# A decode block on one core: VectorE's score loop takes all 32 groups in halves, and the sums free the key slot

## The chip, the cores and the metric

The kernel runs on one core of a Trainium2 chip. The metric is the device time of one execution in microseconds (us), as a median of several runs. 1 MB is a million bytes here; the sizes of single DMAs are in KB of 1024 bytes, as the profile gives them.

## The reference

Four tokens (one for each of B = 4 sequences) pass through two branches that are added. Branch A is attention over a cache: H = 32 heads, S = 4096 cached positions, head width DH = 128, model width D = 512, all float32. Branch B is an MLP; with a single token for each sequence its spatial-shift mixing adds nothing (every shift moves in zeros), so w1 and w2 are not needed. Cut to what is computed:

```
xn  = layernorm(x)
q   = (xn @ wq) by heads
p   = softmax(q . k_cache * DH**-0.5)          # 4 x 32 heads, 4096 positions each
att = (p . v_cache) @ wo
x1  = xn                                        # the shifted mixing is zero for one token
mlp = x1 + gelu(layernorm(x1) @ w3) @ w4
out = x + att + mlp
```

The two caches are 268 MB each; nearly all that the kernel reads is in them, and each element is used once.

## The kernel before, in words

The 128 pairs of sequence and head are taken in NJ = 32 groups of four heads (G = 4). A group's keys are one block of 8.39 MB, 64 KB in each of 128 partitions (R = 128 cached positions of DH = 128 numbers), and its values are another such block. SBUF holds three such slots: two for keys, `ks[0]` and `ks[1]`, used in turn, and one for values, `vs`. The weights borrow the slots: w3 lies in `vs` and wq in `ks[1]` at the start, the values of the last group in `ks[0]`, w4 in `vs` and wo in `ks[1]` at the end.

A group goes through four engines:

- **VectorE (DVE)**, function `scores`, L294 to L330: it fetches the group's query (`qg`, L307) and spreads it over the partitions (`qb`, L308), waits for the keys (`take`, L309), multiplies them in place by the query (L314), sums each row of 128 into a score (`sc`, L315), and finds the negated maximum by head (L319 to L321), which signals `nm`.
- **ScalarE (ACT)**, loop at L335: it waits for `nm`, takes four exponentials into `pw` (L340), signals `go`; later it copies the results out of PSUM (L345, L347) and signals `done`.
- **TensorE (PE)**, function `values`, L367: it takes `go`, signals `expd` (the scores of the group are consumed, L369), waits for the values, and multiplies weights by values (L374, 64 matmuls in the trace's counting) and the normalisers (L379, L381).
- **SyncE (SP)**, L271 to L284, issues nearly all DMAs, in an order written out by hand. SP waits for a semaphore ahead of each load, so a load that is not free to go holds back the ones written behind it.

SP's order is: w3, wq, keys 0; keys 1 (after the q projection has read wq); values 0; keys 2 in two halves; values 1; and from then on keys j+2 and values j+1 in turn. The last loads are values 31 (into `ks[0]`), w4 and wo in five parts. I call the loads k0, k1, ... and v0, v1, ... after their group, and k2a and k2b the halves of k2. Keys j+2 wait for `expd` of group j, which TensorE gives only after VectorE's maxima and ScalarE's four exponentials; values j+1 wait for `done` of group j:

```
load(ks[j % 2], rows(kf, j + 2), f"k{j % 2}", None, EXPD[j])
load(vs, rows(vf, j + 1), "landed", None, DONE[j])
```

On VectorE the groups are not all in the loop. Group 0 is written out ahead of it and works in two halves of R/2 = 64 rows; its first half signals `half`, which frees the first half of the slot for k2a. Group 1 is written out as well, in one piece. Then VectorE waits for k2a (`half_in`, L327) and enters the loop (L329), which takes groups 2 to 31, two in each of 15 iterations, in one piece each:

```
scores([qT[:, 0]], halves=True)
scores([qT[:, 1]])
do.wait("DVE", [half_in])
with nc.Fori(1, NJ // 2, engines=OrderedEngineSet([DVE]), head_slot={DVE: 0}) as j:
```

`take` waits for a semaphore and then lowers it by as much; inside `scores` each instruction waits for the one ahead of it through the semaphore `dve`. `head_slot` says at which slot of a block of instructions the loop's first instruction is placed.

Of the kernel before, what the change touches and what calls it, by code (L numbers as in the profile page):

```python
# [41 lines left out]
AX = mybir.AxisListType  # L42
# [7 lines left out]
PE, DVE, ACT = mybir.EngineType.PE, mybir.EngineType.DVE, mybir.EngineType.Activation  # L50
# [36 lines left out]
def decode_block(ctx: ExitStack, tc: tile.TileContext, x, k, v, wq, wo, w3, w4, out):  # L87
    nc = tc.nc
    B, H, S, DH = k.shape
# [5 lines left out]
    R = G * S // P  # L95
    NG = R // 4
    NJ = B * H // G
# [3 lines left out]
    LAST = NJ - 1  # L101
# [4 lines left out]
    def sb(name, *shape):  # L106
        return consts.tile([P, *shape], F32, name=name)
# [4 lines left out]
    ks = [sb(f"ks{n}", R * DH) for n in range(2)]  # L112
# [11 lines left out]
    gT = sb("gT", NF, B)  # L124
    qT = sb("qT", NJ, DH // HP)
    qg = sb("qg", DH // HP)
    qb = sb("qb", DH)
    sc = [sb(f"sc{n}", R) for n in range(2)]
# [13 lines left out]
    kf = k.rearrange("b h s d -> (b h s d)")  # L142
    vf = v.rearrange("b h s d -> (b h s d)")

    def rows(flat, j):
        n = G * S * DH
        return flat[j * n:(j + 1) * n].rearrange("(p n) -> p n", p=P)

    def blocks4(start, stop, w, m, src):
# [5 lines left out]
    do = Steps(tc)  # L155
    sems = {n: tc.alloc_semaphore(n) for n in (
        "x", "w3", "wq", "k0", "k1", "landed", "last", "w4", "go", "pv", "copied", "poz", "out",
        "half", "half_in", "nm", "dve", "expd", "done")}
    wo_sems = [tc.alloc_semaphore(f"wo{n}") for n in range(5)]
    wo_sb = ks[LAST % 2].rearrange("p (c n) -> p c n", c=WC)  # L160
    wo_cuts = ((0, 16), (16, 24), (24, 28), (28, 31), (31, WC))
# [1 line left out]
    g4 = vs[:, NF * D:NF * D + 4 * 32].rearrange("p (m i) -> p m i", m=4)  # L163

    def load(o, i, sem, by, *after, queue="SP"):
        return do(queue, lambda e: e.dma_start(o, i), *after, done=(sems[sem], 16, by))

    with tc.tile_critical():
# [63 lines left out]
        for c in range(NC):  # L232
            for t in range(4):
                up = lambda e: e.matmul(y[32 * t:32 * t + 32, :FT], x1nT[:, c, :], w3_sb[:, c, t * FT:(t + 1) * FT],
                                        start=(c == 0), stop=(c == NC - 1))
                d = do("PE", up)
# [3 lines left out]
        d = do("DVE", lambda e: e.tensor_mul(u, hs, hs), a)  # L240
        d = do("DVE", lambda e: e.tensor_scalar(u, u, GELU_B, 1.0, op0=ALU.mult, op1=ALU.add), d)
        d = do("DVE", lambda e: e.tensor_mul(u, u, hs), d)
        a = do("ACT", lambda e: e.activation(th, u, AF.Tanh, scale=GELU_A), d)
        d = do("DVE", lambda e: e.tensor_scalar(th, th, 1.0, 0.5, op0=ALU.add, op1=ALU.mult), a)
        d = do("DVE", lambda e: e.tensor_mul(hs, hs, th), d)
        d = do("DVE", lambda e: e.transpose(gt, hs), d)
        gT_ok = do("DVE", lambda e: e.tensor_copy(gT, gt.rearrange("p (m i) -> p m i", i=32)[:, :, 0:B]), d)
# [4 lines left out]
        for c in range(NC):  # L252
            for n in range(2):
                for h in range(G):
                    q = lambda e: e.matmul(pq[n][HP * h:HP * h + HP, :], xnT[:, c, :], wq_h[:, c, n, h],  # L255
                                           start=(c == 0), stop=(c == NC - 1))
                    pq_ok = do("PE", q)
        for n in range(2):
            a = do("ACT", lambda e: e.mul(pw_row[:, n * 4 * DH:(n + 1) * 4 * DH], pq[n], DH ** -0.5), pq_ok)  # L259
        d = do("DVE", lambda e: e.transpose(wide, pw_row), a)  # L260
        pw_ok = do("POOL", lambda e: e.memset(pw, 0.0), d)
        qT_ok = do("DVE", lambda e: e.tensor_copy(
            qT.rearrange("p (b i) n -> p b i n", b=B),
            wide.rearrange("p (i n m) -> p m i n", n=DH // HP, m=32)[:, 0:B]), d)

        EXPD = [(sems["expd"], j + 1) for j in range(NJ)]
        DONE = [(sems["done"], j + 1) for j in range(NJ)]
        HALF = R * DH // 2  # L270
        load(ks[1], rows(kf, 1), "k1", None, pq_ok)  # L271
        load(vs, rows(vf, 0), "landed", None, gT_ok, qT_ok, total_ok)
        half_in = load(ks[0][:, :HALF], rows(kf, 2)[:, :HALF], "half_in", 16, (sems["half"], 1))
        load(ks[0][:, HALF:], rows(kf, 2)[:, HALF:], "k0", None, EXPD[0])
        for j in range(LAST - 1):
            if j > 0:
                load(ks[j % 2], rows(kf, j + 2), f"k{j % 2}", None, EXPD[j])
            load(vs, rows(vf, j + 1), "landed", None, DONE[j])
        last_in = load(ks[(LAST - 1) % 2], rows(vf, LAST), "last", 16, EXPD[LAST - 1])
        w4_in = load(w4_sb, w4.rearrange("(p m) n -> p m n", m=NF), "w4", 16, DONE[LAST - 1])  # L280
        do.wait("SP", [EXPD[LAST]])
        wo_r = wo.rearrange("(p c) n -> p c n", c=WC)
        for (c0, c1), sem in zip(wo_cuts, wo_sems):
            nc.sync.dma_start(wo_sb[:, c0:c1], wo_r[:, c0:c1]).then_inc(sem, 16)  # L284
        d = do("POOL", lambda e: e.memset(g4, 0.0), DONE[LAST - 1])
        g4_ok = do("POOL", lambda e: e.tensor_copy(g4[:, :, 0:B], gT[:, 0:4, :]), d, gT_ok)

        def take(engine, sem, n=1):

            engine.wait_ge(sems[sem], n)  # L290
            engine.sem_inc(sems[sem], -n)  # L291


        def scores(groups, halves=False):  # L294
            n = 0

            def step(i, done="dve"):
                nonlocal n
                if n:
                    i.wait_op(sems["dve"], n, "sem-ge")  # L300
                i.then_inc(sems[done], 1)
                n += done == "dve"

            e = nc.vector
            for s, q in enumerate(groups):
                s = s if len(groups) > 1 else 1 - halves
                step(e.tensor_copy(qg, q))  # L307
                step(e.transpose(qb.rearrange("p (n m) -> p n m", m=HP), qg.unsqueeze(2).to_broadcast([P, DH // HP, HP])))  # L308
                take(e, f"k{s}", 16)  # L309

                w = R // 2 if halves else R
                for c in range(0, R, w):
                    kt = ks[s].rearrange("p (c d) -> p c d", c=R)[:, c:c + w]
                    step(e.tensor_tensor(out=kt, in0=kt, in1=qb.unsqueeze(1).to_broadcast([P, w, DH]), op=ALU.mult))  # L314
                    step(e.reduce_sum(sc[s][:, c:c + w], kt, axis=AX.X), "half" if c + w < R else "dve")  # L315
                if halves:
                    e.wait_ge(sems["half"], 1)
                rm, nm = small[:, s, 0:1], small[:, s, 1:2]
                step(e.reduce_max(rm, sc[s], axis=AX.X))  # L319
                step(e.transpose(tr[s], rm.to_broadcast([P, HP])))  # L320
                step(e.tensor_reduce(nm, tr[s], axis=AX.X, op=ALU.max, negate=True), "nm")  # L321
            take(e, "dve", n)

        do.wait("DVE", [qT_ok])
        scores([qT[:, 0]], halves=True)
        scores([qT[:, 1]])
        do.wait("DVE", [half_in])  # L327
        pairs = qT.rearrange("p (j s) n -> p s j n", s=2)
        with nc.Fori(1, NJ // 2, engines=OrderedEngineSet([DVE]), head_slot={DVE: 0}) as j:  # L329
            scores([pairs[:, s, bass.ds(j, 1)].rearrange("p o n -> p (o n)") for s in range(2)])  # L330


        do.wait("ACT", [pw_ok, rs0])
        ozs = oz.rearrange("p n (j s h) -> p s n j h", s=2, h=G)
        with nc.Fori(0, NJ // 2, engines=OrderedEngineSet([ACT]), head_slot={ACT: 0}) as j:  # L335
            for s in range(2):
                take(nc.scalar, "nm")
                for h in range(G):
                    hp = slice(HP * h, HP * h + HP)
                    i = nc.scalar.activation(  # L340
                        pw[hp, :, 4 * h:4 * h + 4], sc[s][hp, :].rearrange("p (g w) -> p g w", w=4), AF.Exp,
                        bias=small[hp, s, 1:2], scale=1.0, accum_out=rs[hp, h:h + 1])
                i.then_inc(sems["go"], 1)
                take(nc.scalar, "pv")
                nc.scalar.copy(os, pv.rearrange("p (m d) -> p m d", m=4)).then_inc(sems["copied"], 1)  # L345
                take(nc.scalar, "poz")
                nc.scalar.copy(ozs[:, s, :, bass.ds(j, 1)].rearrange("p n o h -> p n (o h)"),  # L347
                               poz[:, 0:2 * G].rearrange("p (n h) -> p n h", n=2)).then_inc(sems["done"], 1)
# [39 lines left out]
        for b in range(B - 1):  # L388
            d = do("PE", lambda e: e.matmul(xb[:, b, :], lts[:, b].rearrange("p h q -> p (h q)"), sel, start=True, stop=True),  # L389
                   LTS[b])  # L390
# [4 lines left out]
        for m in range(NF):  # L395
            t, g, n = (m, g4[:, m, :], 32) if m < 4 else (m % 4, gT[:, m, :], B)
            nc.tensor.matmul(y[32 * t:32 * t + n, :], g, w4_sb[:, m, :], start=(m < 4), stop=False)
        d = do("PE", lambda e: e.matmul(xb[:, B - 1, :], lts[:, B - 1].rearrange("p h q -> p (h q)"), sel, start=True,
                                        stop=True), LTS[B - 1])
# [6 lines left out]
        for (c0, c1), sem in zip(wo_cuts, wo_sems):  # L406
            do.wait("PE", [(sem, 16)])
            for c in range(c0, c1):
                if c < 24:
                    t = (c + 2) % 4  # L410
                    i = nc.tensor.matmul(y[32 * t:32 * t + B, :], X[:, c, :], wo_sb[:, c], start=False, stop=(c >= 20))  # L411
                else:
                    i = blocks4(False, c == WC - 1, X[:, c, :], B, wo_sb[:, c])
            d = do("PE", lambda e: i)
# [7 lines left out]
        d = do("DVE", lambda e: e.tensor_copy(r, total), d)  # L422
        for t in range(4):
            stored = do("SP" if t % 2 == 0 else "ACT", lambda e: e.dma_start(
                out.rearrange("b s d -> (b s) d")[:, P * t:P * t + P], r[32 * t:32 * t + B, :]), d,
                done=(sems["out"], 16, 64))
# [31 lines left out]
```

## Time and profile before

| what | value |
|---|---|
| median of 3 runs | 1309.27 us (1308.49 to 1309.91) |
| the profiled execution: its own time | 1308.19 us |
| its span, from the first instruction to the last | 1306.3 us |
| read from HBM | 561.00 MB |
| DMA queue of SP (q1), share of 16 DMA engines over the span | 99.4% |
| VectorE busy | 1154.5 us (88%) |
| TensorE busy (weight loads beside it) | 366.6 us (28%) (131.6 us, 10%) |
| ScalarE busy | 93.1 us (7%) |
| GpSimd busy | 2.4 us |
| VectorE waiting for keys (L314, from its own sequencer's wait) | 70.6 us in 24 waits |
| mean of one multiply and of one sum over a whole group | 17.23 us, 17.22 us |
| mean of one multiply and of one sum over half a group | 8.69 us, 8.69 us |

The time of the profiled execution is 1.9 us more than its span. "Busy" counts the stretches in which an engine executes; "idle before" in the profile's groups is the time an engine stood still just before an instruction, with the event that ended it. DMA shares are of 16 DMA engines together. In the timeline, a row gives start, duration, engine, line, operation and tiles; SPq rows are the DMAs that SP issues (the duration is that of issuing, not of the transfer).

### The profile page before, as it was taken

The numbers are of one execution on the slowest core, as the hardware profiler recorded it, in microseconds if no ns is written. First come the engines' busy times: TensorE is split into PE (matmuls) and PEld (weight loads), VectorE is DVE, ScalarE is ACT, GpSimd is POOL, SyncE is SP. The second block draws the span as 40 slices with busy tenths as digits, with TensorE's granted clock in tenths as the row PEclk, the third lists the DMA queues.
The fourth block names the chain that finished last, engine by engine and source line by source line (L and its number), as shares of the span: only waits on it lengthen the run. The fifth ranks groups of instructions, "written<-read, shape, count | busy, mean of one in ns | idle before, by whom it ended". The sixth has DMA issues, their size and how long they took to land. (4 is left out here: it accounts for less than half of the span.)

```text
span 1306.3 us, 6535 instructions
## 1 busy us (share of the span) xinstructions
PE 366.6 (28%) x2652; PEld 131.6 (10%) x2652; DVE 1154.5 (88%) x262; ACT 93.1 (7%) x330; POOL 2.4 (0%) x12
## 2 busy tenths in 40 slices
PE   3221233321232321133231123322123333113337
PEld 1000111100111100011110011110001110001112
DVE  3498999999999999999999999999999999999990
ACT  1000000000000000000000000000000000000000
POOL 0000000000000000000000000000000000000000
PEclk8656666655666655666665666665566665566668
DMA  9999999999999999999999999999999999999998
GB/s 402 445 420 431 428 407 439 429 437 433 433 435 431 435 431 435 431 435 431 435 431 435 431 435 431 435 431 435 431 435 431 435 431 435 431 435 431 435 423 347
DMA packets 10561, 561.12 MB, mean 430 GB/s; under 512 B 1188, under 2 KB 1204, under 8 KB 1464
## 3 DMA queue, kind: packets, MB, share of 16 engines
q1 hardware_dynamic: 10528, 561.00, 99.4%
q8 instruction: 4, 0.07, 0.0%
q14 instruction: 5, 0.04, 0.0%
q10 hardware_dynamic: 24, 0.01, 0.0%
HBM read 561.00 MB, written 0.01 MB: 429 GB/s over the span
## 5 line engine op out<-in xcount | busy, mean ns | idle before, releaser
L314 DVE TENSOR_TENSOR ks<-ks,qb 128x16384 f32<-128x16384 f32 (+1 forms) x33 | 551.3, 16707 | 70.9 <-DVEq L291 70.6
L315 DVE TENSOR_REDUCE sc<-ks 128x128 f32<-128x16384 f32 (+1 forms) x33 | 551.2, 16703 | 1.1
L374 PE MATMUL pv<-vs,pw 128*32 128x512 f32 x1984 | 282.7, 734 | 875.7 <-PEq L291 875.7
L374 PEld LDWEIGHTS pv<-vs,pw 128*32 128x32 f32 x1984 | 77.9, 132 | 1055.9 <-issue 1055.9
L345 ACT COPY os<-pv 128x512 f32<-128x512 f32 x32 | 18.8, 586 | 837.7 <-ACTq L291 837.7
L340 ACT ACTIVATE pw<-sc,small 32x128 f32<-32x128 f32 x128 | 51.0, 398 | 266.4 <-ACTq L291 265.2
L379 PE MATMUL poz<-sel,os 128*128 128x4 f32 x256 | 32.8, 252 | 28.2 <-PEq L291 28.2
L379 PEld LDWEIGHTS poz<-sel,os 128*128 128x128 f32 x256 | 31.0, 191 | 56.3 <-issue 56.3
L340 ACT ACTIVATION_READ_ACCUMULATOR pw<-sc,small 32x1 f32 x128 | 23.5, 184 | 0.0
L260 DVE STREAM_TRANSPOSE vs<-pw 128x1024 f32<-128x1024 f32 x1 | 1.2, 1246 | 17.2 <-ACT pw L259 17.2
L422 DVE COPY sc<-total 128x128 f32<-128x128 f32 x1 | 0.3, 290 | 17.5 <-PE total L152 17.5
L307 DVE COPY qg<-qT 128x4 f32 (+1 forms) x32 | 5.4, 170 | 10.1 <-issue 10.1
L355 DVE RECIPROCAL rz<-oz 128x96 f32<-128x96 f32 (+1 forms) x2 | 1.1, 553 | 12.5 <-ACT oz L347 12.4
L381 PE MATMUL poz<-rs,ones 128*128 128x4 f32 x64 | 11.7, 253 | 0.0
L308 DVE STREAM_TRANSPOSE qb<-qg 128x128 f32<-128x128 f32 x32 | 10.0, 311 | 1.1
L319 DVE TENSOR_REDUCE small<-sc 128x1 f32<-128x128 f32 x32 | 9.2, 286 | 1.1
L381 PEld LDWEIGHTS poz<-rs,ones 128*128 128x128 f32 x64 | 9.7, 192 | 0.0
L255 PE MATMUL pv<-ks,X 128*32 128x512 f32 x32 | 5.9, 827 | 11.2 <-DMA ks<-in_A_wq_dram 11.2
L347 ACT COPY oz<-poz 128x8 f32 x32 | 5.3, 166 | 50.9 <-ACTq L291 50.9
L411 PE MATMUL y<-ks,X 128*4 128x512 f32 x48 | 7.3, 772 | 4.6 <-DMA ks<-in_A_wo_dram 4.6
L374 PE MATMUL pv<-ks,pw 128*32 128x512 f32 x64 | 8.3, 676 | 0.1
L320 DVE STREAM_TRANSPOSE tr<-small 128x32 f32<-128x32 f32 x32 | 6.8, 212 | 1.1
(72 smaller groups left out, 68.8 us busy)
## 6 DMA issues: line engine op xcount, KB each, us to landing
ks<-in_A_k_cache_dram SPq DMA_DIRECT2D x2, 4096.0 KB, 25.5
vs<-in_B_w_dram SPq DMA_DIRECT2D x2, 3584.0 KB, 13.9
ks<-in_A_wo_dram SPq DMA_DIRECT2D x1, 4096.0 KB, 19.8
ks<-in_A_wo_dram SPq DMA_DIRECT2D x1, 2048.0 KB, 24.3
ks<-in_A_wo_dram SPq DMA_DIRECT2D x1, 1024.0 KB, 26.3
ks<-in_A_wo_dram SPq DMA_DIRECT2D x1, 768.0 KB, 27.7
ks<-in_A_k_cache_dram SPq DMA_DIRECT2D x31, 39.6
vs<-in_A_v_cache_dram SPq DMA_DIRECT2D x31, 27.1
```

The costliest lines, as they stand in the source:

```text
L255: q = lambda e: e.matmul(pq[n][HP * h:HP * h + HP, :], xnT[:, c, :], wq_h[:, c, n, h], start=(c == 0), stop=(c == NC - 1))
L308: step(e.transpose(qb.rearrange("p (n m) -> p n m", m=HP), qg.unsqueeze(2).to_broadcast([P, DH // HP, HP])))
L314: step(e.tensor_tensor(out=kt, in0=kt, in1=qb.unsqueeze(1).to_broadcast([P, w, DH]), op=ALU.mult))
L315: step(e.reduce_sum(sc[s][:, c:c + w], kt, axis=AX.X), "half" if c + w < R else "dve")
L319: step(e.reduce_max(rm, sc[s], axis=AX.X))
L320: step(e.transpose(tr[s], rm.to_broadcast([P, HP])))
L340: i = nc.scalar.activation(pw[hp, :, 4 * h:4 * h + 4], sc[s][hp, :].rearrange("p (g w) -> p g w", w=4), AF.Exp, bias=small[hp, s, 1:2], sc ...
L345: nc.scalar.copy(os, pv.rearrange("p (m d) -> p m d", m=4)).then_inc(sems["copied"], 1)
L374: i = nc.tensor.matmul(pv[32 * t:32 * t + 32, :], pw[:, g, :], vt[:, 4 * g:4 * g + 4, :], start=(g < 4), stop=(g >= NG - 4))
L379: nc.tensor.matmul(poz[:, 0:G], os[:, m, :], sel.rearrange("p (h m) -> p m h", m=4)[:, m, 0:G], start=(m == 0), stop=(m == 3))
L381: nc.tensor.matmul(poz[:, G:2 * G], ones.to_broadcast([P, P]), rs, start=True, stop=True).then_inc(sems["poz"], 1)
L411: i = nc.tensor.matmul(y[32 * t:32 * t + B, :], X[:, c, :], wo_sb[:, c], start=False, stop=(c >= 20))
```

## The change

VectorE has one loop for all 32 groups, 16 iterations of two groups, entered right after the queries are ready. Every group works in two halves of 64 rows. After each half's sum VectorE waits for that sum and raises a new semaphore, `summed`, by one. The loads of keys wait for `summed` at 2j + 2 (both halves of group j summed) instead of `expd` of group j; so does the load of v31, and so do the five parts of wo at the end (`summed` of the last group). The two halves of k2 wait for the first and second half of group 0.

What protected the scores `sc` from being overwritten before, namely that the keys came late, is now a wait of its own: VectorE takes `expd` ahead of each group's keys. GpSimd (POOL) gives the first two of these at the start. GpSimd also waits for the two halves of k2 and then raises `k0` by 16 on their behalf, so that VectorE's loop can wait for k2 as for any other keys. The loops of VectorE and ScalarE get `head_slot` 128 instead of 0. TensorE's code is unchanged. The core of the diff:

```diff
-        EXPD = [(sems["expd"], j + 1) for j in range(NJ)]
+        SUMMED = [(sems["summed"], 2 * j + 2) for j in range(NJ)]
...
-        half_in = load(ks[0][:, :HALF], rows(kf, 2)[:, :HALF], "half_in", 16, (sems["half"], 1))
-        load(ks[0][:, HALF:], rows(kf, 2)[:, HALF:], "k0", None, EXPD[0])
+        parts = [load(ks[0][:, n:n + HALF], rows(kf, 2)[:, n:n + HALF], f"half{i}", 16, (sems["summed"], i + 1))
+                 for i, n in enumerate((0, HALF))]
         for j in range(LAST - 1):
             if j > 0:
-                load(ks[j % 2], rows(kf, j + 2), f"k{j % 2}", None, EXPD[j])
+                load(ks[j % 2], rows(kf, j + 2), f"k{j % 2}", None, SUMMED[j])
             load(vs, rows(vf, j + 1), "landed", None, DONE[j])
-        last_in = load(ks[(LAST - 1) % 2], rows(vf, LAST), "last", 16, EXPD[LAST - 1])
+        last_in = load(ks[(LAST - 1) % 2], rows(vf, LAST), "last", 16, SUMMED[LAST - 1])
...
-        do.wait("SP", [EXPD[LAST]])
+        do.wait("SP", [SUMMED[LAST]])
...
+        nc.gpsimd.sem_inc(sems["expd"], 2)
+        do.wait("POOL", parts)
+        nc.gpsimd.sem_inc(sems["k0"], 16)
...
+        with nc.Fori(0, NJ // 2, engines=OrderedEngineSet([DVE]), head_slot={DVE: 128}) as j:
+            e, n = nc.vector, 0
...
+            for s in range(2):
+                step(e.tensor_copy(qg, pairs[:, s, bass.ds(j, 1)].rearrange("p o n -> p (o n)")))
                 step(e.transpose(qb.rearrange("p (n m) -> p n m", m=HP), qg.unsqueeze(2).to_broadcast([P, DH // HP, HP])))
+                take(e, "expd")
                 take(e, f"k{s}", 16)
-                w = R // 2 if halves else R
+                w = R // 2
                 for c in range(0, R, w):
                     kt = ks[s].rearrange("p (c d) -> p c d", c=R)[:, c:c + w]
                     step(e.tensor_tensor(out=kt, in0=kt, in1=qb.unsqueeze(1).to_broadcast([P, w, DH]), op=ALU.mult))
-                    step(e.reduce_sum(sc[s][:, c:c + w], kt, axis=AX.X), "half" if c + w < R else "dve")
-                if halves:
-                    e.wait_ge(sems["half"], 1)
+                    step(e.reduce_sum(sc[s][:, c:c + w], kt, axis=AX.X))
+                    e.wait_ge(sems["dve"], n)
+                    e.sem_inc(sems["summed"], 1)
...
-        do.wait("DVE", [qT_ok])
-        scores([qT[:, 0]], halves=True)
-        scores([qT[:, 1]])
-        do.wait("DVE", [half_in])
...
-        with nc.Fori(0, NJ // 2, engines=OrderedEngineSet([ACT]), head_slot={ACT: 0}) as j:
+        with nc.Fori(0, NJ // 2, engines=OrderedEngineSet([ACT]), head_slot={ACT: 128}) as j:
```

More of the change, by code (lines that the diff above doesn't have):

```diff
@@ L157, in decode_block @@
         "x", "w3", "wq", "k0", "k1", "landed", "last", "w4", "go", "pv", "copied", "poz", "out",
-        "half", "half_in", "nm", "dve", "expd", "done")}
+        "half0", "half1", "nm", "dve", "summed", "expd", "done")}
     wo_sems = [tc.alloc_semaphore(f"wo{n}") for n in range(5)]
@@ L284, in decode_block @@
             nc.sync.dma_start(wo_sb[:, c0:c1], wo_r[:, c0:c1]).then_inc(sem, 16)
-        d = do("POOL", lambda e: e.memset(g4, 0.0), DONE[LAST - 1])
-        g4_ok = do("POOL", lambda e: e.tensor_copy(g4[:, :, 0:B], gT[:, 0:4, :]), d, gT_ok)
         def take(engine, sem, n=1):
@@ L291, in take @@
             engine.sem_inc(sems[sem], -n)
-        def scores(groups, halves=False):
-            n = 0
+        nc.gpsimd.sem_inc(sems["expd"], 2)
+        do.wait("POOL", parts)
+        nc.gpsimd.sem_inc(sems["k0"], 16)
+        d = do("POOL", lambda e: e.memset(g4, 0.0), DONE[LAST - 1])
+        g4_ok = do("POOL", lambda e: e.tensor_copy(g4[:, :, 0:B], gT[:, 0:4, :]), d, gT_ok)
+        do.wait("DVE", [qT_ok])
+        pairs = qT.rearrange("p (j s) n -> p s j n", s=2)
+        with nc.Fori(0, NJ // 2, engines=OrderedEngineSet([DVE]), head_slot={DVE: 128}) as j:
+            e, n = nc.vector, 0
             def step(i, done="dve"):
@@ L302, in step @@
                 n += done == "dve"
[L304 to L307, printed above, removed]
+            for s in range(2):
+                step(e.tensor_copy(qg, pairs[:, s, bass.ds(j, 1)].rearrange("p o n -> p (o n)")))
                 step(e.transpose(qb.rearrange("p (n m) -> p n m", m=HP), qg.unsqueeze(2).to_broadcast([P, DH // HP, HP])))
+                take(e, "expd")
                 take(e, f"k{s}", 16)
-                w = R // 2 if halves else R
+                w = R // 2
                 for c in range(0, R, w):
@@ L322, in scores @@
             take(e, "dve", n)
-        do.wait("DVE", [qT_ok])
-        scores([qT[:, 0]], halves=True)
-        scores([qT[:, 1]])
-        do.wait("DVE", [half_in])
-        pairs = qT.rearrange("p (j s) n -> p s j n", s=2)
-        with nc.Fori(1, NJ // 2, engines=OrderedEngineSet([DVE]), head_slot={DVE: 0}) as j:
-            scores([pairs[:, s, bass.ds(j, 1)].rearrange("p o n -> p (o n)") for s in range(2)])
         do.wait("ACT", [pw_ok, rs0])
         ozs = oz.rearrange("p n (j s h) -> p s n j h", s=2, h=G)
-        with nc.Fori(0, NJ // 2, engines=OrderedEngineSet([ACT]), head_slot={ACT: 0}) as j:
+        with nc.Fori(0, NJ // 2, engines=OrderedEngineSet([ACT]), head_slot={ACT: 128}) as j:
             for s in range(2):
```

## The prediction

> **What bounds the kernel now.** I begin with the profile's slices of the span and its table of DMA queues.
>
> ```profile
> DMA  9999999999999999999999999999999999999998
> GB/s 402 445 420 431 428 407 439 429 437 433 433 435 431 435 431 435 431 435 431 435 431 435 431 435 431 435 431 435 431 435 431 435 431 435 431 435 431 435 423 347
> q1 hardware_dynamic: 10528, 561.00, 99.4%
> ```
>
> The transfers are the bound, not VectorE with its 88%: SP's queue keeps the 16 DMA engines busy for 99.4% of the span. In the regular part a group's 16.78 MB take 38.7 us (434 GB/s), so one load of 8.39 MB takes 19.35 us. 561.00 MB at 434 GB/s are 1292.6 us. Of the span of 1306.3 us only 13.7 us are thus open to any change, and the first packet (2.0 us in) and the tail after the last landing (1301.7 to 1306.3) hold half of that. The rest must be places where the DMA engines ran short. The slices wobble early (420, 428, 407), so next come stretches of one group's length, 38.69 us (the last column is GB/s):
>
> ```profile
> 71.31:110.00 38.69, 10.29 (x74) 3.65 (x74) 38.45 (x9) 2.71 (x10) 0.00 (x0) 0.63 1.00 434
> 110.00:148.69 38.69, 9.68 (x74) 3.60 (x74) 32.81 (x8) 2.71 (x10) 0.00 (x0) 0.63 1.00 424
> 148.69:187.38 38.69, 10.37 (x74) 3.71 (x74) 38.48 (x8) 2.71 (x10) 0.00 (x0) 0.63 0.98 417
> 187.38:226.07 38.69, 10.88 (x74) 3.83 (x74) 38.14 (x8) 2.71 (x10) 0.00 (x0) 0.59 1.00 434
> ```
>
> Two stretches are short: 10/434 and 17/434 of 38.69 us, 0.9 and 1.5 us, together **2.4 us**. The third view is the timeline of SP's issues there.
>
> ```profile
> 102.69 0.33 SPq L166 DMA_DIRECT2D vs<-in_A_v_cache_dram  x1
> 126.09 0.33 SPq L166 DMA_DIRECT2D ks<-in_A_k_cache_dram  x1
> 140.85 0.33 SPq L166 DMA_DIRECT2D vs<-in_A_v_cache_dram  x1
> 167.59 0.33 SPq L166 DMA_DIRECT2D ks<-in_A_k_cache_dram  x1
> 181.12 0.33 SPq L166 DMA_DIRECT2D vs<-in_A_v_cache_dram  x1
> ```
>
> These are v1, k3, v2, k4, v3. A load lands in 16 parts, one from each DMA engine. By the DMA records the first part of v1 was in at 127.18 and the last at 129.32. k3 was issued at 126.09, 1.1 us ahead of the first engine's running dry; several engines then stood still for one to two us. k4 came at 167.59, 0.9 us after the first engine had finished v2 (166.65), and all 16 stood still for some time; their next packets took 2.8 to 3.6 us instead of 2.42. v1, issued 5.2 us ahead of k2b's first part (107.86), caused no gap. The last parts landed at 129.32, 149.68, 169.01, 189.60, 208.93: steps of 20.36, 19.33, 20.59, 19.33 us, so the last engine lost 1.0 and 1.25 us, **2.3 us** in all. Why the keys come late is in VectorE's timeline:
>
> ```profile
> 78.47 8.69 DVE L315 TENSOR_REDUCE sc<-ks 128x64 f32<-128x8192 f32 x1
> 87.19 0.29 DVE L319 TENSOR_REDUCE small<-sc 128x1 f32<-128x128 f32 x1
> ...
> 88.44 17.23 DVE L314 TENSOR_TENSOR ks<-ks,qb 128x16384 f32<-128x16384 f32 x1
> 105.70 17.22 DVE L315 TENSOR_REDUCE sc<-ks 128x128 f32<-128x16384 f32 x1
> 122.95 0.29 DVE L319 TENSOR_REDUCE small<-sc 128x1 f32<-128x128 f32 x1
> 123.27 0.21 DVE L320 STREAM_TRANSPOSE tr<-small 128x32 f32<-128x32 f32 x1
> 123.52 0.19 DVE L321 TENSOR_REDUCE small<-tr 128x1 f32<-128x32 f32 x1
> 129.38 0.17 DVE L307 COPY qg<-qT 128x4 f32 x1 [5.67 <-issue]
> ```
>
> The sums of group 1 end at 122.92 and k3 goes at 126.09: maxima, four exponentials and the semaphore through TensorE cost 3.2 us. Then VectorE stands still for 5.67 us at the loop's entry, with keys 2 long landed (k2b at 109.97) and nothing it waits for; the DMA records have an instruction packet in this stretch, at 127.27, and one at 133.33. That delays group 2 and so k4.
>
> **The change, step by step.**
>
> *Keys freed by the sums.* The issue moves forward by the 3.2 us (k4: 164.41 to 167.59, the same). For k2b it is hidden: v0's parts land only from 88.49 on, and k2a lies between. In the regular part it is hidden too: the keys issued at 1195.26 queue 18.7 us ahead of the preceding load's first landing (1213.99). At the end wo goes some 3 us ahead of 1272.68, but w4, issued at 1266.28 and landing 16.5 us later, is still in front of it: nothing.
>
> *The loop entered at 45 us.* The 5.67 us before group 2 go. At the new place VectorE is ready at 45.06 and in the trace waits for k0 until 52.43. An entry as dear as now ends at 50.73; copy and transpose of the query take 0.52 us more, to 51.3. So it is hidden, with 1.1 us to spare. A cheaper one is hidden anyway.
>
> *Halves.* Four half instructions take 34.76 us (52.43 to 87.19), two whole ones 34.51 (88.44 to 122.95): +0.25 a group.
>
> *New waits on VectorE.* Three a group: two waits for a sum with a step of `summed`, and the take of `expd`. The trace has no such row alone. Nearest rows: a take of keys already landed fits into 0.04 us (88.40 to 88.44); a take with register work and the loop's branch is 0.34 us (200.95 to 201.29). A gain is excluded, since nothing is removed for them. I take 0.1 each, nearer to the first since no branch is in them: 0.3 a group, at most 1.0. Behind these waits queue the next half's multiply and, through `nm`, ScalarE and TensorE. A group goes from 35.95 (mean of 36.16 and 35.75, from multiply to multiply at 165.68, 201.84, 237.59) to 36.5 us, at most 37.2, against 38.7 of DMA. The 2.2 us left over hide it; without that cover 32 x 0.55 = 18 us would show.
>
> *`expd` itself* never holds: group 2 asks at 125, and TensorE is past group 0's `go` when its matmuls begin (91.12). *GpSimd between k2 and VectorE* adds its wake-up after the landing at 110, 15 us before group 2 asks. Its two steps ahead lie behind the memset that ends at 44.98, before k0 lands; its later work waits until 1266. SP's order of loads is unchanged.
>
> *The sum.* Group 0's sums end at 87.4. The small instructions and the query take 1.25 us (87.19 to 88.44), the take 0.1; group 1 then runs from 88.75 to 123.7 with its steps, and k3 goes at **123.7** instead of 126.09, 3.5 us ahead instead of 1.1 (2.2 at the dearest waits). Group 2 starts at 125.4 (1.35 and 0.34 for the turn of the loop) and frees its slot at **160.3** instead of 167.59, 5.5 us ahead of v2's first part (then 165.8) instead of 0.9 behind. v1 goes at 103.0 instead of 102.69, still 4.9 ahead. v2 waits on v1's landing as now, 5.7 ahead. Then each group adds 2.2 us of lead. So both gaps close; what is late next is nothing but the transfers.
>
> How much of the 2.3 to 2.4 us arrives at the end? The engines do not lose alike: the first part of k4 is 3.2 us behind a gapless count (127.18 + 58.05 = 185.2, against 188.44), the slowest engine of v1 only 1.2 (129.32 + 58.05 = 187.4; followed packet by packet it ends k4 at 188.6). The gaps had let the others wait for the laggards, and the spread of the parts shrank from 2.1 to 1.2 us. Without gaps the laggards stay last. So the end gains 1.2 to 3.2 us; I take **2.1**, a little under the last landing's 2.3. The profiled execution goes from 1308.19 to 1306.1; the median stands 1.08 above it, so **1307.2 us** (-0.16%).
>
> **The rivals.** *(A) Only one gap closes*, time 1308.0. The shortest lead, 3.5 us for k3, lies between 1.1 (a gap) and 5.2 (none). With an entry 1 to 2 us dearer than its row or waits at 0.3 it falls to 1.5 to 2.2, and k3's 1.0 us stays; k4 keeps 3 us or more. Against: VectorE's start has the 1.1 us to spare.
>
> *(B) The entry is not covered and the gap only moves*, 1309.7. ScalarE enters its loop at the same moment (GpSimd's memset ends at 44.98), and with all DMA engines full the two fetches may stand one behind the other. A doubled entry of 11.3 us puts the first multiply at 56.9, 4.5 late: v1 and k3 then go with leads near 0.4 and lose some 2.7 us in place of the 2.3. For it: between 44 and 57 us there already are two such packets (50.43 and 55.89), which VectorE, written out there, would have no use for. Against: no row shows two fetches delaying each other. [...]
>
> [...]
>
> *(D) The early engines' gain counts*, 1306.3: 3 us arrive.
>
> **How the numbers follow.** Forecast 0.60, A 0.14, B 0.06, C 0.08, D 0.12. About 0.2% (2.6 us) is what a measurement of this kernel can tell from no change. The forecast, with 0.6 us of noise either way, passes it one time in four; with most of D that makes 0.26 faster. C and a little of B make 0.09 slower, and 0.65 lie between. The range runs from 1305.6 (D's 3.2 us and some noise) to 1309.6 (A, most of B); outside are C and the edges.
>
> **What would show it.** Right: all 38.69 us stretches between 71 and 226 at 434 GB/s; the loop's first multiply at 52.4; SP's issues of k3 and k4 near 123.7 and 160.3; VectorE waiting for keys at most groups from some ten groups on, 2 us each; a group's VectorE time near 36.5. Wrong: a first multiply after 53.5, a gap left at 127, idle time at each turn of the loop, or a span that keeps its length though the stretches are at 434, which would put the loss at the tail.

## The result and the profile after

The changed kernel takes **1305.12 us** (median of 7 runs, 1305.01 to 1305.30) against 1309.21 for the kernel before (7 runs, 1308.03 to 1309.91): ratio 0.997, 95% interval 0.9958 to 0.9982. It is 4.1 us faster, 0.31%. The forecast was 1307.2 with a range from 1305.6; the time lies below that range. The profiled execution went from 1308.19 to 1305.01 us, its span from 1306.3 to 1303.1.

The stretches of 38.69 us that were short in the kernel before, in the changed one (last column GB/s):

```profile
71.31:110.00 38.69, 11.13 (x74) 3.88 (x74) 38.19 (x10) 2.71 (x10) 0.00 (x0) 0.59 1.00 434
110.00:148.69 38.69, 10.52 (x74) 3.74 (x74) 37.85 (x10) 2.71 (x10) 0.00 (x0) 0.63 1.00 434
148.69:187.38 38.69, 9.95 (x74) 3.56 (x74) 38.19 (x10) 2.71 (x10) 0.00 (x0) 0.63 1.00 434
187.38:226.07 38.69, 11.07 (x74) 3.83 (x74) 37.84 (x11) 2.71 (x10) 0.00 (x0) 0.59 1.00 434
```

Both holes (424 and 417) are filled. SP's issues in the timeline, v1 to v3 as before:

```profile
103.09 0.33 SPq L166 DMA_DIRECT2D vs<-in_A_v_cache_dram  x1
123.40 0.33 SPq L166 DMA_DIRECT2D ks<-in_A_k_cache_dram  x1
141.25 0.33 SPq L166 DMA_DIRECT2D vs<-in_A_v_cache_dram  x1
160.16 0.33 SPq L166 DMA_DIRECT2D ks<-in_A_k_cache_dram  x1
179.38 0.33 SPq L166 DMA_DIRECT2D vs<-in_A_v_cache_dram  x1
```

k3 goes at 123.40 and k4 at 160.16, forecast at 123.7 and 160.3. VectorE's timeline shows why:

```profile
42.92 1.05 DVE L262 COPY qT<-vs 128x128 f32<-128x128 f32 x1
44.76 0.17 DVE L311 COPY qg<-qT 128x4 f32 x1 [0.78 <-DVE qT L262]
...
51.99 8.69 DVE L320 TENSOR_TENSOR ks<-ks,qb 128x8192 f32<-128x8192 f32 x1 [6.72 <-DVEq L288]
...
124.03 0.19 DVE L328 TENSOR_REDUCE small<-tr 128x1 f32<-128x32 f32 x1
124.55 0.17 DVE L311 COPY qg<-qT 128x4 f32 x1 [0.34 <-issue]
```

The loop is entered with 0.78 us of idle time instead of 5.67, and at 124 there is only the turn of the loop, 0.34 us.

The finest view is the landing of each load, from the trace's DMA records: 16 parts, one from each DMA engine. The table gives the step of the mean part and of the last part from one landing to the next; a load without a hole takes 19.35. "Lost", below, is a step's excess over that. "Lead" is the time from a load's issue to the first landed part of the load ahead of it, which is when the first engine runs dry.

| load, kernel | lead us | step of the mean part | step of the last part |
|---|---|---|---|
| k3, before | 1.1 | 20.53 | 20.37 |
| k4, before | -0.9 | 21.17 | 20.59 |
| k3, changed | 3.8 | 19.35 | 19.35 |
| k4, changed | 5.8 | 19.35 | 19.35 |

A hole is more than standing still. At k4 of the kernel before, the first packet starts at 168.54, 0.95 us after the issue; by the mean of the 16 engines 1.06 us pass without a packet, and the packets that follow are slow, the first of each engine taking 2.7 to 3.6 us instead of 2.42, which adds 0.76. At k3 the engines stand still for 0.45 us on the mean, and slow packets add 0.72.

### The profile page after: what moved, and what is told of

Read it like the earlier page. It is cut to its first block, busy times and chain, and to the rows that moved or that the text cites. A ratio compares the mean times of both kernels' runs of the same rounds, so it can differ in the third digit from the quotient of the medians.

```text
span 1303.1 us, 6697 instructions
## 1 busy us (share of the span) xinstructions
PE 366.4 (28%) x2652; PEld 131.4 (10%) x2652; DVE 1164.2 (89%) x324; ACT 93.1 (7%) x330; POOL 2.4 (0%) x12
## 5 line engine op out<-in xcount | busy, mean ns | idle before, releaser
L320 DVE TENSOR_TENSOR ks<-ks,qb 128x8192 f32<-128x8192 f32 x64 | 556.3, 8692 | 60.4 <-DVEq L288 55.4
L321 DVE TENSOR_REDUCE sc<-ks 128x64 f32<-128x8192 f32 x64 | 555.9, 8686 | 2.2
L311 DVE COPY qg<-qT 128x4 f32 x32 | 5.4, 170 | 5.5 <-issue 4.7
```

Source lines behind the costliest of these rows:

```text
L311: step(e.tensor_copy(qg, pairs[:, s, bass.ds(j, 1)].rearrange("p o n -> p (o n)")))
L321: step(e.reduce_sum(sc[s][:, c:c + w], kt, axis=AX.X))
```

## The experiments

Theory G: the gain is the two stretches in which DMA engines ran dry, and their length differs between executions. Rival F: what goes beyond the forecast comes from fewer instruction packets (packets that the DMA records list under the kind "instruction", 8 or 16 KB each) and from which engine they fall on. Besides the theories, the main parts of the change are undone one after another. The experiments ran on three chips, on each of which the kernel before was timed as well: 1309.43, 1308.49 and 1308.70 us by the median. The changed kernel was timed again only beside the last experiment (1305.13); elsewhere "above the changed kernel" compares with the 1305.12 of the result, and so may hold some tenths of a us that belong to the chip.

**The kernel before, again.** No edit.

> The kernel before, unchanged, profiled once more. Theory G (all of the gain is the two stretches in which the DMA engines ran dry, and how long they stand still differs from one execution to the next): 1309.2 us with a spread of 1.5 to 2 us over the runs; the new profile has its lost transfer time again only at k3 and k4, and more than the first one's 2.3 us if its own time is nearer to 1309 than to 1308. Rival F (the gain beyond 2.3 us comes from fewer instruction packets at the start and from which DMA engine they fall on): k3 and k4 lose the same 2.3 us again and the slowest engine differs elsewhere, in the first 60 us or in the last 30.

Measured: 1309.30 us (1307.95 to 1310.03). Its profiled execution took 1309.30 us, right at the median, where the first took 1308.19. The two short stretches:

```profile
110.00:148.69 38.69, 10.09 (x74) 3.66 (x74) 32.26 (x8) 2.71 (x10) 0.00 (x0) 0.63 1.01 427
148.69:187.38 38.69, 10.62 (x74) 3.74 (x74) 38.48 (x8) 2.71 (x10) 0.00 (x0) 0.59 0.97 412
```

The second hole is deeper than in the first profile (412 against 417). In the landings k3 lost 0.9 us by the mean part and 1.3 by the last, k4 2.2 and 2.8, though k4 was issued with nearly the same lead as in the first profile (-0.95 against -0.93). Then came something that the first profile lacked: k5, v4 and k6 took 19.47, 19.72 and 19.48 us by the mean part, some 0.6 us more in all, with the engines busy and single packets slower (up to 2.75 us). So the holes vary, as G said; the late slow packets were in neither theory.

**Keys freed by the weights again**, all else as changed (k2's second half, v31 and wo wait for `freed` likewise):

```diff
-                load(ks[j % 2], rows(kf, j + 2), f"k{j % 2}", None, SUMMED[j])
+                load(ks[j % 2], rows(kf, j + 2), f"k{j % 2}", None, FREED[j])
...
             nc.tensor.sem_inc(sems["expd"], 1)
+            nc.tensor.sem_inc(sems["freed"], 1)
```

> The changed kernel, but keys j+2, v31 and wo wait again until TensorE has taken the weights of group j (one more semaphore step on TensorE). Theory G: k3 goes near 126.8 instead of 123.4, 0.4 us ahead of the first engine's running dry, and costs 1 to 1.6 us; k4 goes near 163.4, 3 us ahead, and costs nothing: 1306.1 to 1306.7. Rival F: the instruction packets are those of the changed kernel, so 1305.1 to 1305.4.

Measured: 1306.45 us (1305.98 to 1307.59), inside G's range, 1.3 above the changed kernel. SP's issues:

```profile
126.78 0.33 SPq L166 DMA_DIRECT2D ks<-in_A_k_cache_dram  x1
141.70 0.33 SPq L166 DMA_DIRECT2D vs<-in_A_v_cache_dram  x1
163.53 0.33 SPq L166 DMA_DIRECT2D ks<-in_A_k_cache_dram  x1
```

k3 with a lead of 0.5 us lost 0.8 us by the mean part; k4 with 3.4 lost nothing (19.33). F's 1305.1 to 1305.4 is refuted. In this profile (1306.00 us, one of the fastest of its runs) the loss reaches the end by another way than G said: at v31 the last part is only 0.15 us behind that of the changed kernel, and 0.9 are added at w4, whose last part comes 9.39 us after v31's instead of 8.51, with an instruction packet of 16 KB at 1277.5.

**Groups 0 and 1 ahead of the loop again**, in halves, the loop entered at group 2:

```diff
-        with nc.Fori(0, NJ // 2, engines=OrderedEngineSet([DVE]), head_slot={DVE: 128}) as j:
+        def two(queries):
...
+        two([qT[:, 0], qT[:, 1]])
+        with nc.Fori(1, NJ // 2, engines=OrderedEngineSet([DVE]), head_slot={DVE: 0}) as j:
...
```

> The changed kernel, but groups 0 and 1 are written out ahead of VectorE's loop (halves and all), which is entered at group 2 as in the kernel before, at slot 0. Theory G: k3 goes at 123.4 without a gap; the entry costs 5 to 6 us near 124, so k4 goes near 165.5, 0.3 us ahead of v2's first part, and costs 1 to 1.6 us: 1306.1 to 1306.8. Rival F: two more instruction packets, up to 0.5 us: 1305.1 to 1305.6, whenever k4 goes.

Measured: 1308.31 us (1307.84 to 1308.78), 3.2 us above the changed kernel: the right sign for G, twice its size. VectorE and SP:

```profile
124.08 0.19 DVE L328 TENSOR_REDUCE small<-tr 128x1 f32<-128x32 f32 x1
131.77 0.17 DVE L311 COPY qg<-qT 128x4 f32 x1 [7.51 <-issue]
```

```profile
123.45 0.33 SPq L166 DMA_DIRECT2D ks<-in_A_k_cache_dram  x1
141.92 0.33 SPq L166 DMA_DIRECT2D vs<-in_A_v_cache_dram  x1
167.38 0.33 SPq L166 DMA_DIRECT2D ks<-in_A_k_cache_dram  x1
```

The entry cost 7.51 us, not 5 to 6. In the kernel before the instruction packet came at 127.27, when an engine had just run dry because k3 was late; here k3 is in time, and the packet came only at 129.7. In both, the loop's first instruction follows 2.1 us after that packet (129.38, 131.77), so what differs is how late the packet comes; why it comes later is not shown. So k4 went 1.5 us after the first engine had run dry instead of 0.3 ahead, and lost 2.8 us by the mean part. v4 and k6 again had late slow steps (19.68 and 19.55).

**The loops' place.**

```diff
-        with nc.Fori(0, NJ // 2, engines=OrderedEngineSet([DVE]), head_slot={DVE: 128}) as j:
+        with nc.Fori(0, NJ // 2, engines=OrderedEngineSet([DVE]), head_slot={DVE: 0}) as j:
...
-        with nc.Fori(0, NJ // 2, engines=OrderedEngineSet([ACT]), head_slot={ACT: 128}) as j:
+        with nc.Fori(0, NJ // 2, engines=OrderedEngineSet([ACT]), head_slot={ACT: 0}) as j:
```

> The changed kernel with head_slot 0 for the loops of VectorE and ScalarE, as before. Theory G: VectorE's entry now stalls by some 5 us at 44, still inside its wait for k0 (first multiply within 0.5 us of 52.0), no gap opens: 1305.1 to 1305.5. Rival F: at least two more instruction packets between 44 and 60 us, each holding one engine back by 0.6 us: 1305.5 to 1306.3.

Measured: 1305.70 us (1305.61 to 1305.89), 0.6 above the changed kernel, in F's range (near its lower end) and not in G's. VectorE's entry:

```profile
43.65 1.05 DVE L262 COPY qT<-vs 128x128 f32<-128x128 f32 x1
52.01 0.17 DVE L311 COPY qg<-qT 128x4 f32 x1 [7.31 <-issue]
52.22 0.31 DVE L312 STREAM_TRANSPOSE qb<-qg 128x128 f32<-128x128 f32 x1
52.56 8.69 DVE L320 TENSOR_TENSOR ks<-ks,qb 128x8192 f32<-128x8192 f32 x1
```

The entry costs 7.31 us and is almost hidden (multiply at 52.56 against 51.99). No hole opened: k3 had 3.3 us of lead, and every step from k3 on is 19.35. What is lost is at the slowest engine: four instruction packets of 8 KB lie between 48 and 56 us instead of two, in pairs on the same two engines (k1's last part takes 19.92), and v1's last part lands at 129.52 against 128.87, the run's last at 1299.57 against 1298.73. So F is a part of the truth, worth some 0.6 us as far as two chips can be compared.

**The kernel before with one argument changed.**

```diff
-        with nc.Fori(1, NJ // 2, engines=OrderedEngineSet([DVE]), head_slot={DVE: 0}) as j:
+        with nc.Fori(1, NJ // 2, engines=OrderedEngineSet([DVE]), head_slot={DVE: 128}) as j:
```

> The kernel before with one argument changed: head_slot 128 for VectorE's loop, still entered at group 2. Theory G: if the entry then costs 0.8 us as in the changed kernel instead of 5.7, k3 goes as before (126.1, a gap of 0.8 to 1.2 us) and k4 goes near 162.8, 4 us ahead, without a gap: 1306.2 to 1307.0, with a spread of 1 to 2 us because one gap is left. [...] Rival F: two instruction packets less, at most 0.5 us: 1308.8 or more whatever the entry costs.

Measured: 1306.59 us (1305.83 to 1307.48) against 1308.49 for the kernel before there, ratio 0.9984 (0.9975 to 0.9993). The entry at 123.5 cost 0.67 us:

```profile
123.33 0.19 DVE L321 TENSOR_REDUCE small<-tr 128x1 f32<-128x32 f32 x1
124.19 0.17 DVE L307 COPY qg<-qT 128x4 f32 x1 [0.67 <-issue]
```

k3 (lead 1.3) still lost 0.9 us by the mean part; k4 went at 162.40, 4.4 us ahead, and lost nothing (19.39). One number in an argument is worth 1.9 us. With the run before, this shows that either of two parts of the change closes the second hole: the early entry does it at slot 0, and slot 128 does it with the entry left late.

**No halves.**

```diff
-        SUMMED = [(sems["summed"], 2 * j + 2) for j in range(NJ)]
+        SUMMED = [(sems["summed"], j + 1) for j in range(NJ)]
...
-        parts = [load(ks[0][:, n:n + HALF], rows(kf, 2)[:, n:n + HALF], f"half{i}", 16, (sems["summed"], i + 1))
+        parts = [load(ks[0][:, n:n + HALF], rows(kf, 2)[:, n:n + HALF], f"half{i}", 16, (sems["summed"], 1))
...
-                w = R // 2
+                w = R
```

> The changed kernel without halves: every group in one piece, one step of summed a group, both halves of k2 wait for group 0's sums. Theory G: VectorE gains 0.4 us a group, which is worth nothing; k2 goes near 86.9, 1.6 us ahead of v0's first part (88.5), a lead like those of k3 before, so one gap of 0.8 to 1.2 us opens there; k3 and k4 go 5 us ahead: 1305.9 to 1306.5, spread 1 to 2 us. Rival F: same instruction packets, so 1305.1 to 1305.4.

Measured: 1306.06 us (1305.36 to 1308.52), 0.9 above the changed kernel, inside G's range. k2's halves go at 86.84, with a lead of 1.7 us; k2a lost 0.8 us by the mean part and 1.7 by the last. All later steps are 19.32 to 19.35, so the halves pay off only in group 0.

**TensorE's loop at slot 128 as well.**

```diff
-        with nc.Fori(0, LAST, engines=OrderedEngineSet([PE]), head_slot={PE: 0}):
+        with nc.Fori(0, LAST, engines=OrderedEngineSet([PE]), head_slot={PE: 128}):
```

> The changed kernel with head_slot 128 for TensorE's loop as well. No theory sees a gap here. Theory G, with its small term for instruction packets: each of TensorE's two early packets (16 KB, at 35.4 and 47.5 us) puts one DMA engine some 1.5 us behind the others for the rest of the run; if they go, the slowest engine ends 0.3 to 0.5 us earlier: 1304.6 to 1304.9; if they stay, 1305.1 to 1305.3. Rival F: packets carry more of the gain than the gaps do, so without them 1304 or less.

Measured: 1305.34 us (1305.05 to 1306.13). The two 16 KB packets stayed and moved (to 37.9 and 99.5 us), every step from k3 on is 19.35, and nothing was gained; there is no better version in this.

**The changed kernel, again.** No edit.

> The changed kernel, unchanged, once more. Theory G: no gap, every landing from k1 to k6 19.35 us after the one before (9.7 for halves), runs within 0.5 us of each other and a median within 0.3 us of 1305.1 on any chip, while the kernel before moves by 1 us between chips and by 2 to 3 us between runs. Against it: a spread of over 1 us, or a step at any landing.

Measured: 1305.13 us (1304.96 to 1305.29) against 1308.70 (1308.38 to 1310.18) there; all steps of the mean part are between 19.34 and 19.40 from k1 on (9.7 for halves). The changed kernel repeats within 0.3 us in both sets of runs, and so does the one with slot 0; the kernels with holes spread over 0.9 to 3.2 us in sets of 7 to 11 runs. TensorE's slot 128 stands between, 1.1 us without a hole in its profile, so holes are not the only source.

**More work on VectorE**, two multiplies of a spare tile in each group (its allocation and one memset at the start are left out here):

```diff
+                for _ in range(2):
+                    step(e.tensor_tensor(out=junk, in0=junk, in1=junk, op=ALU.mult))
                 take(e, "expd")
```

> The changed kernel with two extra multiplies of 128x640 numbers by themselves in each group on VectorE, which leave the output as it is: some 1.65 us a group, 53 us in all. Theory G: a group takes 38.1 us on VectorE, still under the 38.7 of its transfers; k3 goes near 125.1, 2.1 us ahead, and k4 near 163.6, 2.3 us ahead: between the leads that cost something (up to 1.7 us) and those that did not (from 3.3 us on). So either 1305.1 to 1305.5, if 2 us are enough, or 1306 to 1307.5 with steps of some 20 us at k3 and k4, if not; nothing of the 53 us shows otherwise. Rival: VectorE's work itself is on the path: over 1310.

Measured: 1305.69 us (1305.02 to 1307.46), between the two outcomes that were expected. The engines' busy times on its page, then VectorE's costliest groups and the added one, and last the multiplies' group of the changed kernel (after the bar: busy us, mean ns, and idle time before):

```profile
PE 366.7 (28%) x2652; PEld 132.4 (10%) x2652; DVE 1217.7 (93%) x389; ACT 93.0 (7%) x330; POOL 2.4 (0%) x12
```

```profile
L324 DVE TENSOR_TENSOR ks<-ks,qb 128x8192 f32<-128x8192 f32 x64 | 556.3, 8692 | 10.8 <-DVEq L290 5.0
L325 DVE TENSOR_REDUCE sc<-ks 128x64 f32<-128x8192 f32 x64 | 555.9, 8686 | 2.2
L317 DVE TENSOR_TENSOR junk<-junk 128x640 f32<-128x640 f32 x64 | 52.8, 825 | 2.2
```

```profile
L320 DVE TENSOR_TENSOR ks<-ks,qb 128x8192 f32<-128x8192 f32 x64 | 556.3, 8692 | 60.4 <-DVEq L288 55.4
```

52.8 us more of VectorE work make VectorE 93% busy and the median 0.6 us longer. The idle time ahead of the multiplies falls from 60.4 us (changed kernel) to 10.8: the work went into waiting for keys. k3 had a lead of 1.9 us and lost 0.3 by the mean part, k4 had 2.4 and lost 0.03. That gives a scale of leads, by the mean part and from one profile each: 0.5 to 1.7 us cost 0.8 to 1.2, 1.9 costs 0.3, 2.4 and more next to nothing (0.1 at most); a load 0.9 us late costs 1.8 to 2.2 and one 1.5 late 2.8. With a lead of 1.3 to 1.9 us the engines hardly stand still (0.05 to 0.21 us on the mean); nearly all of the loss is slow packets (0.74 us at 1.3, 0.77 at 1.7, 0.22 at 1.9). The profiled execution was one of the faster ones (1305.36), and the runs of this kernel spread over 2.4 us, so 2.4 us of lead may not always be enough; the kernel with 3.3 us spread over 0.3.

## Why the prediction was wrong, point by point

- *The bound and the two holes*: right. The gain closes exactly these, and undoing either cause reopens its own (1.3 us for the sums, 3.2 for the entry). Not all of a hole is engines running dry: at k3 more than half was slow packets (0.72 of 1.18 us by the mean part).
- *The issue times*: right within 0.3 us (123.40 for 123.7, 160.16 for 160.3). The three small waits at 0.1 us fit: from multiply to multiply 36.4 us (51.99 to 88.34) and 36.8 (88.34 to 125.10, with the loop's turn), where 36.5 were forecast.
- *The entry at 45 us*: hidden, as said, but for another reason. "An entry as dear as now ends at 50.73" supposed 5.67 us; at slot 0, with the engines full, an entry cost 7.31 us at this place and 7.51 at the late one, and the 1.1 us to spare would have been gone (with slot 0 the first multiply came at 52.56 instead of 51.99). The changed slot made it 0.78. Why the slot sets the price is not shown by any run.
- *B* did not happen: 0.78 us for the changed entry. *C*, an entry paid at each turn of the longer loop (1317), did not happen either: no run shows a turn that costs an entry, and the turns cost 0.34 us, as now.
- **The step that failed is the last one, "How much of the 2.3 to 2.4 us arrives at the end?"**: 2.1 us taken, and the median placed "1.08 above" the profiled execution. Two sizes were wrong. First, the profiled execution gained 3.2 us: the last part lands at 1298.73 instead of 1301.83. By k4 the slowest engine was 2.7 us earlier (186.92 against 189.60): the 2.3 us of the holes, and 0.4 that it was already ahead at v1 (128.87 against 129.32). 2.5 us are left when v31 lands (1270.60 against 1273.14), and 0.6 are added in the last 30 us. There the kernel before had an instruction packet at 1279.6, after which its slowest engine was 1.2 us behind the mean instead of 0.7; the changed kernel's at 1277.5 did not touch its slowest engine. So "the laggards stay last" held (the spread of the parts stays 1.6 us until wo), but I let it cut the gain below the last landing's own 2.3, where the first and the mean part gave 3. Where the holes had brought the engines closer together, a 16 KB instruction packet in the last 30 us made a new laggard: w4's last part came 9.09 us after v31's in the kernel before instead of 8.51, 9.39 with the keys freed by the weights and 9.83 with the late entry. (In the repeat and in the run without halves the hole left one engine 1.8 to 2.4 us behind the mean instead, and this step was 8.50 to 8.51.) So the end of the kernel before lost about what the mean part lost, and not only what the last part had lost at the holes. Second, 1.08 us is no constant. As far as two profiles show, it is the variation of the holes and of the packets after them: the profiled execution was one of the fastest, and in the repeat, with the median's time, the last part landed 4.4 us later than in the changed kernel (1303.09). The changed kernel's runs lie within 0.3 us, so the median gains 0.9 us more than the profiled execution. The runs of the kernel before, 1.4 us apart, should have been read as part of the loss. The size that was missed is thus 1.1 us in the profiled execution (1305.01 for 1306.1) and 1.0 in the median's distance from it (0.11 for 1.08).
- *The range* reached to D's 3.2 us, counted from one lucky profile, and lacked the variation of 1 us on the side of a larger gain.

Open: why packets are slower 40 to 140 us after a hole at k4 in some executions. In both profiles where k4 lost most (the repeat of before and the late entry), they were; in the first profile, with a smaller loss, they were not. With slot 128 in the kernel before, which has a hole at k3 alone, v3 took 19.42 us, a weaker case of the same. How much of the 0.6 us at slot 0 comes from the number of packets and how much from their falling on the same engines was not tried either.

## What to carry to other kernels

When the transfers fill 99% of a span, count landings, not averages (a load's landing step against the regular one shows each hole), and see by how much each issue leads the end of the load ahead: here leads of 0.5 to 1.7 us still cost 0.8 to 1.2, a lead of 2.4 cost 0.03 in one profile, and the kernel with 3.3 had its runs within 0.3 us. Free a buffer at its last reader (undoing it cost 1.3 us here), and spend a loop's entry where its engine waits anyway (entered late and at slot 0 it cost 3.2). If the runs of a kernel differ by more than those of a kernel without holes, part of the difference can belong to the loss that a change removes (not all of it: one kernel without a hole in its profile spread over 1.1 us), so the gain is to be taken from the median and not from one fast profile.

## What the runs showed of the hardware that was not expected

A loop's entry cost 7.3 to 7.5 us with all DMA engines full, 5.7 and 6.2 in the two profiles of the kernel before, where an engine ran dry meanwhile, and 0.7 to 0.8 with the loop's first instruction at slot 128. In the kernel before, the first packet of k4 started 0.95 us after its issue, with the engines standing free (167.59 to 168.54), and after this hole the first packets took 2.7 to 3.6 us instead of 2.42; with leads of 0.5 to 1.7 us at k3 most of them were slow too (11 to 14 of 16 over 2.6 us). By the DMA records, followed engine by engine, one instruction packet in the first 134 us of the kernels before and after put its DMA engine some 0.6 to 1.5 us behind the others (it took 0.31 to 0.37 us for 8 KB and 1.02 to 1.04 for 16 KB, and the packet of the load behind it 2.7 to 3.1 instead of 2.42), and with no hole to wait in the engine stayed behind: in the changed kernel the last part of a load came 1.1 us after the mean one from k2 to v31.
